# Batch 0 of a fused attention and GEGLU kernel in a new hand-written order, with a longer ring of exponentials and one pair's operands by DMA transposes

## The chip, the core and the metric

The kernel runs on one core of one Trainium2 chip. Its time is the device time in microseconds of one execution, as the median of several runs. The core's engines are TensorE (PE: matrix products and transposes into PSUM; PEld is its loading of stationary operands), VectorE (DVE), ScalarE (ACT), GpSimd (POOL) and SyncE (SP). Each works through its own instructions in their written order, and they wait for each other by semaphores. DMAs that SP issues run in queue q1 of the profile, those that POOL issues in q0.

## The reference

A hash-bucketed attention over 4 batches, 8 heads, 768 positions and a head dimension of 64, followed by a gated feed-forward layer on the 3072 x 512 result:

```python
q_bits = (np.einsum('bhsd,dk->bhsk', q, proj) > 0)      # 6 bits; k_bits alike
mask = q_bucket[:, :, :, None] == k_bucket[:, :, None, :]
scores = np.where(mask, scale * np.matmul(q, k.transpose(0, 1, 3, 2)), -1e9)
attn = softmax(scores)                                  # + 1e-9 in the divisor
x = np.matmul(attn, v)                                  # heads side by side: 3072 x 512
g = x @ w_gate
ffn = (0.5 * g * (1 + erf(g / sqrt(2)))) * (x @ w_val) @ w_out
out = x + ffn / (1 + np.exp(-(x @ w_res)))
```

## The kernel before

The attention is worked in 16 pairs of heads, four to a batch (p = 0 to 15). A pair's q and k are loaded as fp32 (`load`, L75), turned in 32 x 32 blocks by DVE (`tr`, L190), hashed by small fp32 products (`hash_mm`, L197, or `hash_one`, L230, for the first pair), turned back (`hash_tok`, L209) and compared with zero (`bits`, L220). The six bits stand as plus or minus a half beside the 64 columns of a bf16 copy (`cast`, L176) in one of four buffers `nat`; the copy of q is scaled by 1/2048, so that after the product one exponential with a large scale gives both the bucket mask and the score. The operand with its bits is transposed into `aug`: in batch 0 by TensorE (`turn_pe`, L253: six 128 x 128 transposes for one head of one side, into a PSUM bank, and `turned`, L262, copies it out), later by one DMA transpose for both heads (`turn`, L245).

A pair has nine chunks (36 slots to a batch). `scores` (L373) makes a chunk of 128 x 1024 scores in one of two PSUM buffers `sp` and has ACT write its exponential to `e`, a ring of four. `values` (L345) multiplies a chunk's exponentials with v into the PSUM tile `av`; after half of a pair's chunks one head is complete, gets a small uniform term (`preset`, L323, from the sums that `vals_s` makes on POOL) and is divided into `x_tok` (`finish`, L299, on DVE). `finish` also issues a DMA transpose of `x_tok` into `x_sb` for the first two pairs of batch 0; `x_turn` (L335) does the other two on TensorE.

When a batch's attention is done, `gate_val` (L403) makes 12 steps m of gate and value products: both go through the two `sp` buffers, ACT takes the Gelu of the first into `gt`, and DVE multiplies it with the second into `hh` (L419), which frees the second buffer. Work for the next batch's pairs hangs on these steps (`gv_work`). `project` (L425) is spread over the next batch's slots.

The order around all this is written out with slot numbers: `pe(s, ...)` puts a piece behind the scores of slot s, `at(s, ...)` behind the values, `gv(b, m, ...)` behind step m; `loads` and `load_w` (weights, issued by POOL with a cast from fp32, L168) are pieces too. Values follow their scores by two slots (`LAG`). In PSUM, `hash_mm`, q's transposes and the residual products take the bank tagged "r", k's transposes, `htp` and the output products the bank "f".

The lines that set the order of loads, and those in the gate phase of batch 0 for pairs 6 and 7:

```python
loads(s0 + (6 if b == 0 else 2) + 4 * j, (x[0], "qk"[x[1]]))    # x: pairs 4, 5
loads(s0 + (22 if b == 0 else 18) + 3 * j, (y[0], "qk"[y[1]]))  # y: pairs 6, 7
gv(b, 0, lambda p0=p0: tokens((p0, p0 + 1), True))
for m, x in zip((0, 1, 2, 4), xs):
    lay(b, m, x)                                                # bits, then turn
gv(b, 3, lambda y=ys[2]: tr(*y))
gv(b, 5, lambda y=ys[3]: tr(*y))
```

Of the kernel before, what the change touches and what calls it, by code (L numbers as in the profile page):

```python
# [14 lines left out]


@with_exitstack
def kernel(
# [86 lines left out]
    load(1, 0)  # L105
    load_v(0)
    load(1, 1)
    for p in range(2, 4):
        load_v(p - 1)
        load(p, 0)  # L110
        load(p, 1)
# [76 lines left out]
    t32, hsum, htok = {}, {}, {}  # L188

# [7 lines left out]
    def hash_mm(jobs, dhs=(0, 1), hs_=(0, 1)):  # L197
        if jobs[0] not in hsum:
            hsum[jobs[0]] = mm_ps.tile([P, HT, 32], FP32, tag="r", name="hs")
        hs = hsum[jobs[0]]  # L200
        for hh in hs_:
            sl = slice(hh * T, hh * T + T)
            for dh in dhs:
                for j, x in enumerate(jobs):
                    nc.tensor.matmul(hs[32 * j:32 * j + 32, sl], projw[:, dh, :],  # L205
                                     t32[x][:, sl, dh, :], start=(dh == 0), stop=(dh == 1),
                                     tile_position=(0, 32 * j))

    def hash_tok(jobs, psum=False):  # L209
        n = 32 * len(jobs)  # L210
        if psum:
            ht = mm_ps.tile([P, HT, 32], FP32, tag="f", name="htp")
        else:
            ht = sm_pool.tile([P, HT, 32], FP32, tag="ht", name="ht")
        nc.vector.transpose(ht[:n].rearrange("p c n -> p (c n)"),  # L215
                            hsum[jobs[0]][:n].rearrange("p c n -> p (c n)"))
        for j, x in enumerate(jobs):
            htok[x] = (ht, j)

    def bits(p, side, engs=(nc.vector,)):  # L220
        x = (p, side)
        ht, j = htok.pop(x)
        for a in range(4):
            engs[a % len(engs)].tensor_scalar(  # L224
                nat_of(x)[32 * a:32 * a + 32, :, D:D + NBITS],
                ht[32 * j:32 * j + 32, :, NBITS * a:NBITS * (a + 1)], 0.0, 0.5,
                op0=ALU.is_gt, op1=ALU.subtract)


    def hash_one(p, side, hi, pool, tag):  # L230
        hs = pool.tile([P, 2, T, 32], FP32, tag=tag, name="hs1")
        sl = slice(hi * T, hi * T + T)
        for dh in range(2):
            nc.tensor.matmul(hs[:, 0], projs[:, dh, :], t32[p, side][:, sl, dh, :],
                             start=(dh == 0), stop=(dh == 1))
        hsum[p, side, hi] = hs

    def bits_one(p, side, hi):
        hs = hsum.pop((p, side, hi))
        nc.vector.transpose(hs[:, 1].rearrange("p c n -> p (c n)"),  # L240
                            hs[:, 0].rearrange("p c n -> p (c n)"))
        nc.vector.tensor_scalar(nat_of((p, side))[:, hi * T:hi * T + T, D:D + NBITS],
                                hs[:, 1, :, 0:NBITS], 0.0, 0.5, op0=ALU.is_gt, op1=ALU.subtract)

# [7 lines left out]

    def turn_pe(p, side, hi, tag=None, pool=mm_ps):  # L253
        x = (p, side)
        if x not in aug:
            aug[x] = aug_pool.tile([P, HT, P], BF16, tag=f"aug{side}", name=f"aug{side}")
        pt = pool.tile([P, T, P], BF16, tag=tag or "rf"[side], name="pt")
        for t in range(T):
            nc.tensor.transpose(pt[0:KA, t, :], nat_of(x)[:, hi * T + t, 0:KA], ident)  # L259
        pts[p, side, hi] = pt  # L260

    def turned(p, side, hi, eng, t0=0, t1=T):  # L262
# [4 lines left out]
        else:  # L267
            eng.tensor_copy(dst, pt)

# [29 lines left out]
    def finish(p, hi):  # L299
# [4 lines left out]
        o = av.pop((p, hi))  # L304
        rec = sm_pool.tile([P, T], FP32, tag="rec", name="rec")
# [3 lines left out]
        if hi == 1 and (0 < b < B - 1 or hp < HP - (2 if b == 0 else 1)):  # L309
# [6 lines left out]
    def opened(p, hi):  # L316
        if (p, hi) in av:
            return
        av[p, hi] = av_ps.tile([P, T + 1, D + 1], FP32, tag="av", name="av")
# [15 lines left out]
    def x_turn(b, hp):  # L335
        pt = mm_ps.tile([P, T, P], BF16, tag="f" if b == 0 else "r", name="pt")
# [8 lines left out]
    def values(p, c, e):  # L345
        va = vaug[p]
        for i in range(2):
# [12 lines left out]
            if (2 * c + i + 1) % NCH == 0:  # L360
                if p < HP:
                    preset(p, hi)
                if (p, hi) not in late:
                    finish(p, hi)

    pending = []
    late = ((0, 0), (0, 1), (1, 0))
# [5 lines left out]
    def scores(p, c):  # L373
# [10 lines left out]
        e = e_pool.tile([P, 1024], BF16, tag="e", name="e")  # L384
# [5 lines left out]
    hidden = {}  # L390
# [12 lines left out]
    def gate_val(b, begun, beside):  # L403
        for m in range(KF):
            ps = []
            for i, w in enumerate((wg, wv)):
# [5 lines left out]
                if m == 0 and i == 1:  # L412
                    beside()
# [3 lines left out]
            if m == 0:  # L417
# [7 lines left out]
    def project(b):  # L425
        hh = hidden[b]
        for t in range(T):
            last = b == B - 1 and t == T - 1
            rps = mm_ps.tile([P, DMODEL], FP32, tag="r", name="rps")
# [8 lines left out]
            for k0, k1 in ((0, 3), (3, 4)) if last else ((0, KM),):  # L438
                cs = slice(k0 * P, k1 * P)
                if b < B - 1:  # L440
                    fps = mm_ps.tile([P, DMODEL], FP32, tag="f", name="fps")
# [22 lines left out]
    tr(0, 0, 1, 2)  # L464
# [44 lines left out]
    for p in range(HP, NPAIR):  # L509
        for hi, s in enumerate((9 * p - (p % HP == 0), 9 * p + 5)):  # L510
            at(s - 2, lambda p=p, hi=hi: opened(p, hi))
# [23 lines left out]


    at(0, lambda: bits_one(0, 0, 1), lambda: tr(1, 0), lambda: bits_one(0, 1, 1))
    pe(0, lambda: hash_one(0, 1, 1, av_ps, "av"))
    at(1, lambda: tr(1, 1))
    pe(2, lambda: turn_pe(0, 0, 1, "av", av_ps), lambda: turn_pe(0, 1, 1))  # L540
    at(2, lambda: turned(0, 0, 1, nc.vector))
    at(2, lambda: turned(0, 1, 1, nc.vector, 0, 2), lambda: turned(0, 1, 1, nc.vector, 2, T))
    at(2, lambda: tr(2, 0))
    hash_pe((1,), 4, (4,))
    turns_pe(1, (6, 6, 8, 9))
    at(6, lambda: finish(0, 0), lambda: tr(2, 1))
    at(8, lambda: tr(3, 0))
    at(9, lambda: tr(3, 1))
    at(11, lambda: finish(0, 1))
    at(5, lambda: vals_a(1))  # L550
    at(7, lambda: vals_s(1))
    for side in range(2):
        at(4 + side, lambda side=side: cast(2, side, nc.gpsimd))
        at(9 + side, lambda side=side: cast(3, side, nc.gpsimd))
    hash_pe((2, 3), 13, (13, 16))
    turns_pe(2, (15, 15, 17, 18))
    at(15, lambda: finish(1, 0))
    at(13, lambda: vals_a(2))
    at(15, lambda: vals_s(2))
    turns_pe(3, (22, 22, 23, 24))  # L560
    at(18, lambda: vals_a(3))
    at(22, lambda: vals_s(3))
    pe(30, lambda: x_turn(0, HP - 2))
    for i in range(6):
        at(11 + 3 * i, load_w)
    for m in (0, 0, 4, 5, 6, 7):
        gv(0, m, load_w)
    loads(0, (3, "v"))

# [4 lines left out]
    for b in range(B - 1):  # L574
# [3 lines left out]
        for j, (x, y) in enumerate(zip(xs, ys)):  # L578
            at(s0 + 24 + 2 * j, lambda x=x: tr(*x))
            at(s0 + 25 + 2 * j, lambda x=x: cast(*x, nc.gpsimd))  # L580
            if j < 2:
                at(s0 + 32 + 2 * j, lambda y=y: tr(*y))
            loads(s0 + (6 if b == 0 else 2) + 4 * j, (x[0], "qk"[x[1]]))
            loads(s0 + (22 if b == 0 else 18) + 3 * j, (y[0], "qk"[y[1]]))
        gv(b, 0, lambda p0=p0: tokens((p0, p0 + 1), True))
        for m, x in zip((0, 1, 2, 4), xs):
            lay(b, m, x)
        gv(b, 3, lambda y=ys[2]: tr(*y))
        gv(b, 5, lambda y=ys[3]: tr(*y))
        for m, y in zip((5, 5, 6, 6), ys):  # L590
            gv(b, m, lambda y=y: cast(*y, nc.gpsimd))
        gv(b, 6, lambda p0=p0: hashed((p0 + 2, p0 + 3)))
        gv(b, 7, lambda p0=p0: tokens((p0 + 2, p0 + 3), True))
        for m, y in zip((7, 8, 9, 10), ys):
            lay(b, m, y)
    for p in range(HP, NPAIR):
        at(9 * p - 8, lambda p=p: vals_s(p), lambda p=p: vals_a(p))
        loads(9 * p - 20, (p, "v"))
# [13 lines left out]
    for s in range(LAST):  # L612
# [5 lines left out]
        if b >= 1:  # L618
            mlp_mm(AHEAD + (slot + 1) * (NMM - HELD - AHEAD) // NSLOT - done[0])
# [5 lines left out]
        if slot == NSLOT - 1:  # L625
            values(*pending.pop(0))
            ps = (HP * (b + 1), HP * (b + 1) + 1)
            if b == 0:
                nc.scalar.activation(table, warm[:, 0:1], AF.Gelu)
                begun = [gv_mm(0, 0, wg, 0, KM - 1)]  # L630
                values(*pending.pop(0))
                begun.append(gv_mm(0, 0, wv, 0, KM - 1))
                x_turn(b, HP - 1)
                hashed(ps, 0, 3)
                gate_val(b, begun, lambda: hashed(ps, 3, 4))
            else:
                mlp_mm(4)
                flush()
                begun = [gv_mm(b, 0, w, 0, KM - 1) for w in (wg, wv)]
                if b < B - 1:  # L640
                    mlp_mm(NMM)
                    gate_val(b, begun, lambda: hashed(ps))
                else:
                    x_turn(b, HP - 1)
                    mlp_mm(HELD - 7)
                    gv(b, 0, lambda: mlp_mm(NMM))
                    gate_val(b, begun, lambda: mlp_mm(3))
# [35 lines left out]
```

## Time and profile before

| | us |
|---|---|
| time, median of 3 runs (lowest to highest) | 346.99 (346.71 to 347.24) |
| span of the profiled execution, first to last instruction | 344.9 |
| PE busy | 334.2 |
| ACT busy | 206.7 |
| DVE busy | 191.4 |
| POOL busy | 86.3 |
| first exponential of batch 0 starts | 8.49 |
| first Gelu of batch 0 starts | 51.39 |

The profile is one execution. Its page gives the busy time of each engine, and views of the trace give instructions in order of time, groups of equal instructions, what ended each idle time, the chain of waits that ended last, the busy times by stretch and the DMA transfers with the time from issue to landing. A matrix product's end is modelled, so PE's busy share is no measure of how well it is used. Engines that wait for something off the chain cost nothing by it.

### The profile page before, as it was taken

The page shows a single profiled execution, that of the slowest core. Times are in us where ns is not written, and L with a number is a line of the kernel's source. Part 1 is how long each engine was busy: PE and PEld are TensorE (multiplying, and loading weights), DVE is VectorE, ACT ScalarE, POOL GpSimd, SP SyncE. Part 2 cuts the span into 40 slices and gives each one's busy share as a digit, 9 for nine tenths or more (in the row PEclk, how much of TensorE's full clock was granted, in tenths as well). Part 3 has the DMA queues.
Part 4 walks back from the last instruction along what each step waited for, and adds up shares of the span by engine and source line. Part 5 has one row for each costly group of instructions (what it writes and reads, how often), then busy time and mean ns, then how long its engine had stood idle before and what let it go on. Part 6 is the DMA issues. An engine that isn't in the chain of part 4 may idle for free.

```text
span 344.9 us, 7549 instructions
## 1 busy us (share of the span) xinstructions
PE 334.2 (97%) x3064; PEld 204.3 (59%) x3112; DVE 191.4 (56%) x403; ACT 206.7 (60%) x232; POOL 86.3 (25%) x162
## 2 busy tenths in 40 slices
PE   7999999999999999999999999999999999999994
PEld 5667665655666655655666665655566665656442
DVE  7877757755345856757344784747244444333333
ACT  3789973226999962224999982323999984223110
POOL 4779940371055000270044100242030000000000
PEclk9999999999999999999999999999999999999999
DMA  7979999999375833528366642626330220000022
GB/s 224 376 62 219 205 276 217 197 139 193 103 188 172 204 106 78 102 38 149 82 193 188 231 115 65 128 48 113 72 100 32 55 55 30 32 1 0 32 77 76
DMA packets 71171, 42.90 MB, mean 124 GB/s; under 512 B 49504, under 2 KB 68192, under 8 KB 71136
## 3 DMA queue, kind: packets, MB, share of 16 engines
q1 hardware_dynamic: 64720, 37.17, 42.9%
q0 software_dynamic: 6336, 5.24, 10.8%
q8 instruction: 24, 0.39, 0.4%
q14 instruction: 11, 0.09, 0.1%
q10 hardware_dynamic: 80, 0.00, 0.0%
HBM read 29.36 MB, written 6.29 MB: 103 GB/s over the span
## 4 chain that ended last, share of the span: by engine, by line
PE 88%; ACT 4%; DVE 2%; DMA 2%; issue 2%; SPq 1%; POOL 0%; DVEq 0%; ACTq 0%
PE sp L399 36%; PE fps L445 18%; PE sp L380 15%; PE av L354 8%; PE rps L431 6%; ACT e L385 4%; PE hs L205 3%; DMA ld<-in_k_dram 2%; PE pt L259 1%; DVE o L451 1%; DVE nat L224 0%; SPq L96 0%; DVE o L448 0%; DVE ht L215 0%; DVE hh L419 0%
## 5 line engine op out<-in xcount | busy, mean ns | idle before, releaser
L385 ACT ACTIVATE e<-sp 128x1024 bf16<-128x1024 f32 x144 | 143.6, 1027 | 13.5 <-PE sp L380 8.0
L416 ACT ACTIVATE gt<-sp 128x768 bf16<-128x768 f32 x48 | 38.9, 811 | 92.5 <-PE sp L399 92.5
L380 PE MATMUL sp<-aug,aug 71*128 71x256 bf16 (+1 forms) x384 | 86.1, 325 | 1.1 <-ACT e L385 0.6
L445 PE MATMUL fps<-wo,hh 128*128 128x512 bf16 (+2 forms) x274 | 74.7, 369 | 1.6
L419 DVE TENSOR_TENSOR hh<-gt,sp 128x768 bf16<-128x768 bf16 x48 | 45.8, 954 | 50.1 <-PE sp L399 46.1
L399 PE MATMUL sp<-x_sb,wv 128*128 128x512 bf16 (+1 forms) x379 | 70.6, 325 | 0.4 <-DVE hh L419 0.2
L399 PE MATMUL sp<-x_sb,wg 128*128 128x256 bf16 (+1 forms) x373 | 70.4, 324 | 0.7
L354 PEld LDWEIGHTS <-e 128*128 128x128 bf16 x1152 | 53.3, 97 | 28.9 <-issue 1.2
L354 PE MATMUL av<-va,e 128*128 128x65 bf16 x1152 | 58.7, 193 | 0.1
L399 PEld LDWEIGHTS <-wv 128*128 128x128 bf16 x384 | 37.6, 98 | 25.1 <-issue 0.3
L399 PEld LDWEIGHTS <-wg 128*128 128x128 bf16 x384 | 36.8, 98 | 26.2 <-issue 2.3
L445 PEld LDWEIGHTS <-hh 128*128 128x128 bf16 x300 | 27.4, 97 | 22.7 <-issue 0.2
L448 DVE SCALAR_TENSOR_TENSOR o<-th,fps 128x512 f32<-128x512 f32 (+2 forms) x25 | 16.6, 666 | 36.6 <-PE fps L445 31.0
L380 PEld LDWEIGHTS <-aug 71*128 71x128 bf16 x384 | 29.4, 97 | 10.9 <-issue 2.2
L184 POOL TENSOR_SCALAR nat<-ld 128x768 bf16<-128x768 f32 (+1 forms) x16 | 13.8, 861 | 78.0 <-DMA aug<-nat 74.6
L281 POOL TENSOR_TENSOR v<-ldv 128x384 f32<-128x384 f32 x16 | 16.0, 999 | 67.7 <-DMA ldv<-in_v_dram 67.6
L194 DVE STREAM_TRANSPOSE t<-ld 128x768 f32<-128x768 f32 (+1 forms) x34 | 31.0, 916 | 1.4 <-DMA ld<-in_q_dram 0.7
L333 DVE COPY av<-av 128x390 f32<-128x390 f32 x24 | 13.6, 567 | 29.8 <-PE av L329 29.8
L431 PE MATMUL rps<-wr,x_sb 128*128 128x512 bf16 x90 | 25.3, 378 | 0.2
L435 ACT ACTIVATE th<-rps 128x512 f32<-128x512 f32 x24 | 14.2, 594 | 18.4 <-PE rps L431 18.4
L224 DVE TENSOR_SCALAR nat<-htp 32x72 bf16<-32x72 f32 x96 | 21.9, 229 | 1.8
L307 DVE TENSOR_TENSOR x_tok<-av,rec 128x384 bf16<-128x384 f32 x32 | 17.8, 557 | 1.1
(61 smaller groups left out, 190.7 us busy)
## 6 DMA issues: line engine op xcount, KB each, us to landing
ldv<-in_v_dram SPq DMA_DIRECT2D x16, 384.0 KB, 5.4
out_dram<-o SPq DMA_DIRECT2D x23, 256.0 KB, 2.0
ld<-in_q_dram SPq DMA_DIRECT2D x15, 384.0 KB, 5.4
ld<-in_k_dram SPq DMA_DIRECT2D x15, 384.0 KB, 6.2
wg<-in_moe_w_gate_dram POOLq DMA_DIRECT2D x4, 384.0 KB, 10.2
wv<-in_moe_w_val_dram POOLq DMA_DIRECT2D x4, 384.0 KB, 12.2
wo<-in_moe_w_out_dram POOLq DMA_DIRECT2D x3, 512.0 KB, 6.9
wr<-in_moe_w_res_dram POOLq DMA_DIRECT2D x1, 512.0 KB, 14.9
```

The source lines that it names most:

```text
L194: nc.vector.transpose(t32[p, side][:, sl].rearrange("p c h n -> p (c h n)"), raw[p, side][:, sl].rearrange("p c d -> p (c d)"))
L224: engs[a % len(engs)].tensor_scalar(nat_of(x)[32 * a:32 * a + 32, :, D:D + NBITS], ht[32 * j:32 * j + 32, :, NBITS * a:NBITS * (a + 1)], 0 ...
L307: nc.vector.tensor_mul(x_tok[b][:, hp, :, hi * D:(hi + 1) * D], o[:, 0:T, 0:D], rec.unsqueeze(2).to_broadcast([P, T, D]))
L354: nc.tensor.matmul(av[p, hi][:, qt, :], e[:, off:off + P], va[:, hi, jt, 0:D + 1], start=first, stop=(p >= HP and jt == T - 1), skip_group ...
L380: nc.tensor.matmul(sp[:, off:off + nq * P], ks[0:KA, hi * T + jt, :], qs[0:KA, hi * T + qt0:hi * T + qt0 + nq, :], start=True, stop=True)
L385: nc.scalar.activation(e, sp, AF.Exp, scale=float(ALPHA))
L399: nc.tensor.matmul(sp[:, c0:c1], w[:, kk, bass.ts(m, P)], xs[:, kk, c0:c1], start=(kk == 0), stop=(kk == KM - 1))
L416: nc.scalar.activation(gt, sp[:, 0:S], AF.Gelu)
L419: nc.vector.tensor_mul(hidden[b][:, m, :], gt, ps[1][:, 0:S])
L431: nc.tensor.matmul(rps, x_sb[b][:, kk, t, :], wr[:, kk, :], start=(kk == 0), stop=(kk == KM - 1))
L445: nc.tensor.matmul(fps[:, cs], hh[:, m, bass.ts(t, P)], wo[:, m, cs], start=(m == 0), stop=(m == KF - 1))
L448: nc.vector.scalar_tensor_tensor(o[:, cs], th[:, cs], 1.0, fps[:, cs], op0=ALU.add, op1=ALU.mult)
```

## The change

Batch 0's attention leaves the slot loop. Every piece of work gets a name: `s5` and `v5` are the scores and values of chunk 5, `tr41` is `tr` of pair 4, side 1 (k), `h10` to `h13` the four pieces of the second hash, `tk` its turning back, `bt` the comparisons, `tp` and `td` TensorE's transposes and their copies out, `tu` a DMA transpose, `cs` a cast, `ld` and `lv` loads, `va` and `vs` the preparation of v, `w` a weight load, `fin` a finish, `xt` an `x_turn`, `g0` and `g1` the begun first gate and value products. One list gives their order, a second one the pieces beside the 12 steps of batch 0's gate phase. The slot loop starts at batch 1.

```diff
+FIRST_LOADS = [(1, "q"), (0, "v"), (1, "k"), (2, "q"), (2, "k"), (2, "v"), (1, "v"), (3, "k"), (3, "q")]
+HASHES = [(0, (1,)), (1, (2, 3)), (2, (4, 5)), (3, (6, 7))]
+X_PE = 2
+ORDER = """
+trq trk ld41 s0 tdq tdk hoq bo0 ho s1 bo1 tr10 s2 tr11 tp011 cs21 tp001 v0 v1 s3 td011a td011b h00
+h01 td001 s4 s5 h02 h03 ld40 s6 v2 v3 tr20 s7 tr21 v4 tk0 bt10 bt11 tp100 tp110 td100 td110 s8 tr31
+tp111 tr30 lv3 s9 fin00 tp101 td101 ld61 s10 ld50 cs20 v5 v6 v7 v8 fin01 s11 ld51 va2 s12 cs31 h10
+va1 h11 td111 s13 vs1 lv4 h12 h13 s14 v9 v10 cs30 w0 s15 v11 v12 s16 tk1 bt20 bt21 bt31 tp200 tp210
+td200 td210 bt30 tr50 s17 tp201 td201 va4 s18 w1 w2 v13 fin10 vs2 s19 tu31 tp211 td211 cs41 s20 v14
+vs3 s21 v15 tu30 s22 v16 tr40 tr61 v17 s23 tr41 va3 fin11 w3 s24 v18 vs4 s25 v19 v20 v21 s26 cs40
+s27 ld70 v22 v23 fin20 tr51 s28 v24 v25 ld60 s29 v26 fin21 s30 lv5 s31 v27 s32 v28 v29 v30 w4 w5 w6
+cs50 cs51 s33 xt2 s34 v31 fin30 tr60 s35 gelu v32 v33 v34 g0 v35 fin31 g1 xt3 h20 h21 h22 lv6 w7
+op40
+"""
+BESIDE = [
+    "h23 tk2 bt41 tu41 cs61",
+    "bt40 tu40 cs60",
+    "bt50",
+    "bt51 w8 w9 ld71 tr71",
+    "tr70",
+    "tu51 cs71",
+    "h30 h31 h32 h33 tk3 bt61 tu61 tu50",
+    "bt60 w10",
+    "w11",
+    "bt71 tu71",
+    "bt70 cs70 tu70",
+    "pr40 rp40 tu60",
+]
```

The exponentials of batch 0 go to a ring of nine in the tile `hh`, which is free until the gate phase, and TensorE's work takes whichever of the banks "r" and "f" is free:

```diff
+    free_banks, held_banks = ["r", "f"], {}
+    def take(what=None):
+        tag = free_banks.pop(0)
...
+    RING = KF * S // 1024
...
-        e = e_pool.tile([P, 1024], BF16, tag="e", name="e")
+        if p < HP:
+            if 0 not in hidden:
+                hidden[0] = hh_pool.tile([P, KF, S], BF16, tag="hh", name="hh")
+            n = (p * NCH + c) % RING
+            e = hidden[0].rearrange("p m s -> p (m s)")[:, n * 1024:(n + 1) * 1024]
+        else:
+            e = e_pool.tile([P, 1024], BF16, tag="e", name="e")
         nc.scalar.activation(e, sp, AF.Exp, scale=float(ALPHA))
```

At the start, the second head's hash and transposes stand in the list, and ACT copies four of the six blocks of the first operand, DVE the other two. Pair 3 is in the list with `tu30` and `tu31` and without `tp3..`, so its operands come from two DMA transposes:

```diff
-    tr(0, 0, 1, 2)
     cast(0, 0, nc.scalar, 0, 1)
     cast(0, 1, nc.gpsimd, 0, 1)
     bits_one(0, 0, 0)
     turn_pe(0, 0, 0)
     fill(2, 256)
-    turned(0, 0, 0, nc.scalar)
     bits_one(0, 1, 0)
+    turned(0, 0, 0, nc.scalar, 0, 4)
     turn_pe(0, 1, 0)
-    hash_one(0, 0, 1, av_ps, "av")
-    tr(0, 1, 1, 2)
     turned(0, 1, 0, nc.vector, 0, 2)
-    turned(0, 1, 0, nc.vector, 2, T)
...
+    job("gelu", lambda: nc.scalar.activation(table, warm[:, 0:1], AF.Gelu))
+    for i, w in enumerate((wg, wv)):
+        job(f"g{i}", lambda w=w: begun.append(gv_mm(0, 0, w, 0, KM - 1)))
+    for name in ORDER.split():
+        first.pop(name)()
...
+            for m, names in enumerate(BESIDE):
+                for name in names.split():
+                    gv(b, m, first.pop(name))
...
+    gate_val(0, begun)
+    mlp.append(project(0))
+    for s in range(NSLOT, LAST):
```

Batches 1 to 3 keep their order; of pairs 4 to 7 it is the loads, hashes, casts and transposes made during batch 0 that are placed anew.

More of the change, by code (lines that the diff above doesn't have):

```diff
@@ L104 @@
     load_head(0, 1, 1, nc.sync)
[L105 to L111, printed above, removed]
+    for what in FIRST_LOADS:
+        load_v(what[0]) if what[1] == "v" else load(what[0], "qk".index(what[1]))
     warm = const.tile([P, P], BF16, name="warm")
@@ L188, with give, acc, acc_done @@
     t32, hsum, htok = {}, {}, {}
+    free_banks, held_banks = ["r", "f"], {}
+    def take(what=None):
+        tag = free_banks.pop(0)
+        if what is None:
+            free_banks.append(tag)
+        else:
+            held_banks[what] = tag
+        return tag
+    def give(what):
+        if what in held_banks:
+            free_banks.append(held_banks.pop(what))
+    accs = []
+    def acc(what):
+        assert len([x for x in accs if x is not None]) < 2 and (len(accs) < 2 or accs[-2] is None), accs
+        accs.append(what)
+    def acc_done(what):
+        accs[len(accs) - 1 - accs[::-1].index(what)] = None
     def tr(p, side, h0=0, h1=2):
@@ L222, in bits @@
         ht, j = htok.pop(x)
+        n, what = ht_left.pop(id(ht))
+        if n > 1:
+            ht_left[id(ht)] = (n - 1, what)
+        else:
+            give(what)
         for a in range(4):
@@ L411, in gate_val @@
                 ps.append(sp)
-                if m == 0 and i == 1:
+                if m == 0 and i == 1 and beside:
                     beside()
@@ L558, with job @@
[L558 to L568, printed above, removed]
+    first = {}
+    def job(name, fn):
+        first[name] = fn
+    held = []
+    for c in range(HP * NCH):
+        job(f"s{c}", lambda c=c: held.append(scores(*divmod(c, NCH))))
+        job(f"v{c}", lambda: values(*held.pop(0)))
@@ new lines @@
+    for p in range(HP - 1, 2 * HP):
+        job(f"lv{p}", lambda p=p: load_v(p))
+        for side in range(2):
+            job(f"ld{p}{side}", lambda p=p, side=side: load(p, side))
+    for n, ps in HASHES:
+        for i in range(4):
+            job(f"h{n}{i}", lambda i=i, ps=ps: hashed(ps, i, i + 1))
+        job(f"tk{n}", lambda ps=ps: tokens(ps, ps[0] >= HP))
+    for i in range(12):
+        job(f"w{i}", load_w)
+    for hp in range(HP):
+        job(f"xt{hp}", lambda hp=hp: x_turn(0, hp))
@@ L571, in lay @@
+    for what, fn in (("op", opened), ("pr", preset), ("rp", repeat)):
+        job(f"{what}{HP}0", lambda fn=fn: fn(HP, 0))
+    begun = []
+    job("gelu", lambda: nc.scalar.activation(table, warm[:, 0:1], AF.Gelu))
[3 more added lines that the diff above has]
+        first.pop(name)()
     def lay(b, m, x):
```

165 lines of the change are left out of this document (91 added, 74 removed).

## The prediction, made before the changed kernel had run

> **What bounds the kernel now.** I read the page's engine sums first, then the busy times by stage, then ScalarE's timeline through batch 0, because the change touches batch 0 and little else.
>
> ```profile
> PE 334.2 (97%) x3064; PEld 204.3 (59%) x3112; DVE 191.4 (56%) x403; ACT 206.7 (60%) x232; POOL 86.3 (25%) x162
> ```
> ```profile
> 13.39:47.49 34.10, 32.70 (x477) 23.35 (x474) 25.54 (x58) 30.48 (x32) 28.68 (x50) 1.00 1.06 200
> 47.49:51.39 3.90, 3.85 (x51) 2.37 (x51) 1.45 (x4) 1.87 (x3) 0.00 (x0) 1.00 1.18 277
> 51.39:82.56 31.17, 30.85 (x215) 18.41 (x218) 20.60 (x47) 10.17 (x13) 10.32 (x18) 1.00 1.12 189
> ```
>
> The columns after the stretch are its length and the busy time of PE, PE's weight loads, DVE, ACT and POOL, then PE's clock and the share of the DMA engines. PE is at 97% over the span. Batch 0's attention (8.49 to 47.49) is the place where PE is not the plain limit: ACT, PE and, above 1.0, the DMA engines are all close to full. From 51.39 to 82.56 (batch 0's gate and value products) PE sets the time, with the DMA engines still full.
>
> ```profile
> 8.49 4.08 ACT L385 ACTIVATE e<-sp 128x1024 bf16<-128x1024 f32 x4 [0.89 <-PE sp L380]
> 13.39 1.02 ACT L385 ACTIVATE e<-sp 128x1024 bf16<-128x1024 f32 x1 [0.82 <-PE sp L380]
> 14.95 1.94 ACT L385 ACTIVATE e<-sp 128x1024 bf16<-128x1024 f32 x2 [0.54 <-PE sp L380]
> 17.60 5.64 ACT L385 ACTIVATE e<-sp 128x1024 bf16<-128x1024 f32 x6 [0.71 <-PE sp L380]
> 23.72 1.02 ACT L385 ACTIVATE e<-sp 128x1024 bf16<-128x1024 f32 x1 [0.49 <-PE sp L380]
> 25.30 1.94 ACT L385 ACTIVATE e<-sp 128x1024 bf16<-128x1024 f32 x2 [0.55 <-PE sp L380]
> 27.99 6.55 ACT L385 ACTIVATE e<-sp 128x1024 bf16<-128x1024 f32 x7 [0.76 <-PE sp L380]
> 34.80 2.04 ACT L385 ACTIVATE e<-sp 128x1024 bf16<-128x1024 f32 x2 [0.26 <-PE sp L380]
> 37.00 10.47 ACT L385 ACTIVATE e<-sp 128x1024 bf16<-128x1024 f32 x11 [0.16 <-PE sp L380]
> 51.39 0.81 ACT L416 ACTIVATE gt<-sp 128x768 bf16<-128x768 f32 x1 [1.16 <-PE sp L399]
> ```
>
> These 36 exponentials end at 37.00 + 10.47 = 47.47, and the first Gelu comes 3.92 later. Back to back they follow each other by (10.47 - 1.03) / 10 = 0.944 us. The eight gaps in brackets after the first row add up to 4.29 us: that is what a better order can win, plus whatever the first exponential (8.49) can be moved forward. The chain of waits shows what makes a gap.
>
> ```profile
> 14.12 0.59 DVE ht L215
> 15.39 0.20 DVE nat L224
> 15.64 1.01 PE pt L259 x12
> ...
> 16.78 0.17 PE av L326
> ...
> 17.50 0.25 PE av L354 x8
> 17.75 0.44 PE sp L380 x3
> 18.18 0.35 PE pt L259 x6
> ...
> 22.05 0.79 PE hs L205 x16
> ```
>
> A hash goes through DVE (14.12 to 15.59, transpose and six comparisons) while PE holds a 12-fold transpose behind it, in order; the scores stand behind that. The rows also give PE's prices: scores of one chunk 0.44, values 0.25, six transposes 0.35, two hash pieces 0.79, a preset 0.17.
>
> **The change, part by part.** *Removed.* The fourth pair's 24 TensorE transposes (4 x 0.35 = 1.4 us of PE) and four DVE copies:
>
> ```profile
> L268 DVE COPY aug<-pt 71x768 bf16<-71x768 bf16 x13 | 6.7, 542 | 2.2 <-PE pt L259 2.2
> ```
>
> 4 x 0.54 = 2.2 us of DVE. With them gone PE's work from piece s4 to s35 is 32 x 0.44 + 30 x 0.25 + 8 x 0.35 + 6 x 0.40 (hash pieces) + 7 x 0.17 + 0.35 (xt2) = 28.3 us, against 32 x 0.944 = 30.2 us of ACT. So ACT sets the pace there and I book the 1.4 us at nothing by itself: it is cover for the lumps. The ring of nine lets values lag by up to six chunks (s26 is issued when v21 is done); the old ring of four with two in hand could not.
>
> *Start.*
>
> ```profile
> 6.57 0.57 DVE L194 STREAM_TRANSPOSE t<-ld 128x384 f32<-128x384 f32 x1
> 7.15 0.87 PE L234 MATMUL hs<-t,projs 128*128 128x192 f32 x4
> 7.35 0.62 DVE L268 COPY aug<-pt 71x256 bf16<-71x256 bf16 x2 [0.22 <-PE pt L259]
> 7.86 0.60 PE L380 MATMUL sp<-aug,aug 71*128 71x512 bf16 x2
> 11.42 0.20 POOL projw L144
> ```
>
> The first scores (7.86) stood behind a hash of the second head on PE (7.15), and the first comparisons behind a 0.57 transpose on DVE. Both now come after. DVE's first copy moves from 7.35 to about 6.8, s0 to 7.05, the first exponential to 7.05 + (8.49 - 7.86) = 7.7: 0.8 earlier. But s1 now waits for two transposes and two copies on DVE (2 x 0.5 + 0.2 + 0.4 after 6.9, so 8.5), which puts the second exponential at 9.55, a gap of 0.9. The first pair's hash still waits for projw (11.62), two pieces (0.79) and s4 follow it, so the fifth exponential starts at 13.2 against 13.39: a gap of 0.6 and another of 0.15 before it.
>
> *Middle.* Counting PE and DVE forward by the order with the prices above, I find three more gaps that the order leaves: 0.5 at s8 (tk0 and its six comparisons end at 16.15, then 2 x 0.35 and the scores), 0.5 at s11 (v5 to v8 and a preset are 1.17, more than 0.944 - 0.44), and 0.25 in small ones up to s17. Sum of gaps 2.9 in place of 4.29. The last exponential ends at 7.7 + 35 x 0.944 + 1.03 + 2.9 = 44.7 (2.7 earlier). Bounds: with the start's gaps alone (1.65) it is 43.4; with as much as now (4.29) it is 46.1.
>
> *The fourth pair's DMA transposes.* tu31 is ready when its comparisons end, about 26.0, tu30 about 27.8; s27 wants both by 7.7 + 27 x 0.944 + 2.9, less the 0.7 by which scores lead their exponential, that is 35.4. Ahead of them on SP's queue stand x_sb's first transpose, ld51 and lv4; behind them x_sb's second, ld70, ld60, lv5, lv6.
>
> ```profile
> L248 SPq DMA_TRANSPOSE aug<-nat x8: 1433/1682/5029, 54.8 to 82.1; - x8
> ...
> DMA to landing us min/median/max: 3.7/4.1/9.7
> ```
> ```profile
> ldv<-in_v_dram SPq DMA_DIRECT2D x1, 384.0 KB, 7.7
> ```
> ```profile
> q0 software_dynamic: 378, 0.28, 93.7%
> q1 hardware_dynamic: 422, 0.11, 41.1%
> ```
> ```profile
> q1 hardware_dynamic: 1971, 0.50, 123.2%
> ```
>
> The 7.7 is v4's load issued at 25.22 today; its twin lv4 is issued near 24.5, so it lands at 30 to 32. The q rows are 36 to 38 us (weights in q0 against a transpose in q1) and 64 to 66 (transposes alone). An operand is 128 x 12 x 128 x 2 bytes in packets of 256, so 1536 packets: 1.6 us alone (985 per us), 7.3 us beside weights (211 per us). Both transposes alone need 3.1 us after lv4, so 33 to 35, in time; POOL's va4 also waits for lv4 and holds w1 and w2 back, which gives them that window. Bounds: no wait, or 3.5 us (the second rival). I take 0.3, near the lower end, because of that window.
>
> *Tail.* v35, preset, g1, xt3 and three hash pieces follow the last exponential much as now; 3.84 in place of 3.92. First Gelu: 44.7 + 0.3 + 3.84 = 48.9, that is 2.5 earlier.
>
> *Gate phase.* k7's load (ld71) moves from slot 31 to the fourth step of the gate, on SP behind tu41 and tu40, and tr71 needs it at once; behind tr71 on DVE stands the hh product of step 4, which frees PSUM for the next value product, so PE stops about 0.3 us after DVE is late.
>
> ```profile
> 54.82 28.71 SPq L248 DMA_TRANSPOSE aug<-nat  x8
> ```
> ```profile
> 56.10 0.95 DVE L224 TENSOR_SCALAR nat<-htp 32x72 bf16<-32x72 f32 x4
> ...
> 60.32 0.95 DVE L419 TENSOR_TENSOR hh<-gt,sp 128x768 bf16<-128x768 bf16 x1 [0.66 <-PE sp L399]
> 61.19 0.97 DVE L194 STREAM_TRANSPOSE t<-ld 128x768 f32<-128x768 f32 x1
> 62.92 0.95 DVE L419 TENSOR_TENSOR hh<-gt,sp 128x768 bf16<-128x768 bf16 x1 [0.76 <-PE sp L399]
> ```
> ```profile
> ld<-in_q_dram SPq DMA_DIRECT2D x1, 384.0 KB, 3.4
> ```
>
> Relative to the first Gelu (51.39): first transpose issued +3.4, second ready +5.7, step 4's product +11.5. So in the new kernel tu41 is issued at 52.3, tu40 is ready at 54.6, tr71 wants its data at 59.8 (after step 3's product and four comparisons) and step 4 is due at 60.4. The load can be issued once tu40 is off SP: 54.6 + 1.43 at the earliest, 3.77 + 5.03 after 52.3 (the first two issues today) at the latest, and then takes 3.4 alone: 59.5 to 64.5. Weights w4 to w7, issued some 45 to 47, keep q0 full to about 56 and slow tu41, so that tu40's packets end near 59.5 and the load lands about 61.3. Then step 4 starts at 62.4: 2.0 late, 1.6 of it paid by PE (0.3 is slack, 0.1 the late comparisons). Bounds 0 and 4.9.
>
> The remaining pieces (w8 to w11, tu61 to tu60, the opening of pair 4) have 10 us or more before their use: nothing.
>
> **Sum** against the profiled execution (span 344.9, 2.1 less than the median of the runs): -2.7 + 0.3 - 0.1 + 1.6 = -0.9, span 344.0, time 346.1.
>
> **Rivals.**
> (a) The load lands before 59.8, so only the first part counts: -2.5, **344.5**. For it: a lone load took 3.4 and 1.43 is the shortest issue. Against: it needs both transposes through in 5 us while q0 is full. Chance 0.22.
> (b) The fourth pair's transposes are late at s27. w1 and w2 are 512 packets each; sharing turn by turn, 1024 transpose packets go at 211 per us (4.9 us), the other 2048 at 985 (2.1 us): 31 + 7 + 0.9 = 38.9, 3.5 after 35.4. The gate then starts 0.7 later than now and its load is less late (0.5): **348.2**. It decides as soon as w1's packets start before tu31's end. The Trainium skill ("DMA: Bandwidth & Descriptors", section "Queues, rings and completion order") says that a DMA engine takes packets in turn from the queues that have work; the 378 beside 422 above agree. By that rule alone the sum is this rival's wherever the weights overlap the transposes. Chance 0.14.
> (c) Slower: tu41 and tu40 hold SP for 3.77 and 5.03 as today, the load is issued at 61.1 and lands at 64.5, step 4 starts at 65.5 against 62.92 now: +2.3, **349.3**, and more where the load queues longer. From a landing after 62 on it eats the whole gain. For it: the first two issues today were under the same weights. Against: fewer weights are left at that time. Chance 0.22.
> (d) The order only moves the gaps (4.29 remain): the attention ends 1.3 earlier, the load is then 0.8 late for PE, and -1.3 + 0.3 - 0.1 + 0.8 = -0.3: **346.7**, no change. Chance 0.08.
>
> **Numbers.** Forecast 346.1, chance 0.34, its own range 345 to 347.2. What a measurement can tell from no change is 0.2%, 0.7 us. Faster: all of (a), two thirds of the forecast: 0.44. Within: a quarter of the forecast and (d): 0.17. Slower: (b), (c) and the rest: 0.39. The range 343.8 to 350 leaves out a better (a) with fewer gaps, and (c) with a long queue.
>
> **What would show it.** Right: first exponential near 7.7, gaps of the exponentials near 2.9 in sum, the last ending near 45, no PE wait for a DMA at s27, first Gelu near 49, and one DVE wait for ld<-in_k_dram in the gate of 1 to 2 us with PE idle behind it. Wrong: a PE wait on aug at the fourth pair's first scores (b), a wait of 4 us or more in the gate (c), none (a), or exponentials with gaps as now (d). A late ld60 ahead of the attention's last product, which I book at nothing since it should land near 42 and is wanted near 44, would also break it.

## The result and the profile after

| | median us | lowest to highest | executions | ratio to before (95% interval) |
|---|---|---|---|---|
| before | 346.84 | 346.36 to 347.46 | 20 | |
| changed | 348.92 | 345.31 to 350.63 | 20 | 1.0049 (1.0031 to 1.0067) |

The changed kernel is 0.5% slower where the forecast was 346.1, slightly faster. Its spread is five times that of before, and its profiled execution is the shortest of the twenty (345.31, span 343.6): this profile shows what the change can do and hides most of what costs it the time. So I read it first against the steps of the prediction, and then the profile of a longer execution of the same kernel (348.48, span 346.8, the run e_look1 below).

The windows of the changed kernel, with the columns explained in the prediction: attention, its tail, and the gate phase from the first Gelu to the twelfth; the last row is the gate phase of the kernel before.

```profile
8.03:45.08 37.05, 36.09 (x507) 25.40 (x508) 27.61 (x65) 34.26 (x36) 28.51 (x55) 1.00 1.04 248
45.08:48.99 3.91, 3.86 (x51) 2.38 (x51) 1.29 (x4) 1.87 (x4) 2.39 (x4) 1.00 1.26 223
48.99:80.51 31.52, 29.75 (x207) 17.64 (x210) 19.68 (x43) 8.91 (x12) 5.41 (x7) 1.00 1.15 182
```
```profile
51.39:81.29 29.90, 29.58 (x207) 17.62 (x210) 19.89 (x44) 8.92 (x11) 10.32 (x18) 1.00 1.12 188
```

From the first exponential to the end of the last are 37.05 us; before it was 47.47 - 8.49 = 38.98. The tail is as long as it was. The gate phase took 29.90 before and takes 31.52 now, so 1.6 of the gain went there. ScalarE's timeline through batch 0's attention shows the gaps, in brackets:

```profile
8.03 1.02 ACT L459 ACTIVATE hh<-sp 128x1024 bf16<-128x1024 f32 x1 [1.05 <-PE sp L448]
9.98 1.94 ACT L459 ACTIVATE hh<-sp 128x1024 bf16<-128x1024 f32 x2 [0.92 <-PE sp L448]
12.11 1.02 ACT L459 ACTIVATE hh<-sp 128x1024 bf16<-128x1024 f32 x1 [0.19 <-PE sp L448]
13.42 3.77 ACT L459 ACTIVATE hh<-sp 128x1024 bf16<-128x1024 f32 x4 [0.29 <-PE sp L448]
17.66 2.91 ACT L459 ACTIVATE hh<-sp 128x1024 bf16<-128x1024 f32 x3 [0.46 <-PE sp L448]
21.00 2.85 ACT L459 ACTIVATE hh<-sp 128x1024 bf16<-128x1024 f32 x3 [0.44 <-PE sp L448]
24.10 20.98 ACT L459 ACTIVATE hh<-sp 128x1024 bf16<-128x1024 f32 x22 [0.24 <-PE sp L448]
```

Six gaps of 2.54 in sum in place of eight of 4.29; from 24.10 on, 22 exponentials follow each other without one, chunk 27 with pair 3's DMA transposes among them. VectorE's timeline and PE's waits in the gate phase show the late load that was foreseen:

```profile
58.91 0.98 DVE L282 TENSOR_SCALAR nat<-htp 32x72 bf16<-32x72 f32 x4
61.15 0.98 DVE L240 STREAM_TRANSPOSE t<-ld 128x768 f32<-128x768 f32 x1 [1.26 <-DMA ld<-in_k_dram]
62.16 0.95 DVE L492 TENSOR_TENSOR hh<-gt,sp 128x768 bf16<-128x768 bf16 x1
```
```profile
PE sp L472 <- DVE hh L492: 1.5, 1, 1.5
```

k7's load lands at 61.15, DVE waits 1.26 for it, and PE 1.5 behind DVE. SP's timeline has tu41 and tu40, and the load behind them, which landed 3.6 later:

```profile
52.41 5.11 SPq L308 DMA_TRANSPOSE aug<-nat  x2
57.57 0.57 SPq L107 DMA_DIRECT2D ld<-in_k_dram  x1
```

Now the longer execution of the same kernel: the waits of DVE and PE (us in total, times, longest) in its gate phase and the turn to batch 1.

```profile
DVE nat L282 <- DMA aug<-nat: 3.4, 1, 3.4
...
PE fps L518 <- DVE nat L282: 1.5, 1, 1.5
...
PE sp L472 <- DVE hh L492: 0.8, 1, 0.8
...
PE sp L448 <- DVE hh L492: 0.6, 1, 0.6
DVE t L240 <- DMA ld<-in_k_dram: 0.6, 1, 0.6
```

The load costs less here (0.6, and 0.8 of PE). The long wait is another one: DVE's comparisons `bt70` (line 282 writes `nat`) wait 3.4 us for a DMA transpose, and with them the last product of the gate, on which the first output product (line 518) and the scores (line 448) hang. In the short execution this wait was 0.83; the kernel before has none. VectorE's timeline of the long execution, and ScalarE's at the turn to batch 1 in the short execution, in the long one and in the kernel before:

```profile
84.29 0.96 DVE L282 TENSOR_SCALAR nat<-htp 32x72 bf16<-32x72 f32 x4 [3.36 <-DMA aug<-nat]
85.28 0.95 DVE L492 TENSOR_TENSOR hh<-gt,sp 128x768 bf16<-128x768 bf16 x1
```
```profile
82.63 1.02 ACT L459 ACTIVATE e<-sp 128x1024 bf16<-128x1024 f32 x1
83.55 0.59 ACT L508 ACTIVATE th<-rps 128x512 f32<-128x512 f32 x1
84.03 2.87 ACT L459 ACTIVATE e<-sp 128x1024 bf16<-128x1024 f32 x3
```
```profile
83.33 1.02 ACT L459 ACTIVATE e<-sp 128x1024 bf16<-128x1024 f32 x1
84.25 0.59 ACT L508 ACTIVATE th<-rps 128x512 f32<-128x512 f32 x1
86.92 3.00 ACT L459 ACTIVATE e<-sp 128x1024 bf16<-128x1024 f32 x3 [2.08 <-PE sp L448]
```
```profile
83.42 1.02 ACT L385 ACTIVATE e<-sp 128x1024 bf16<-128x1024 f32 x1
```

The second exponential follows the first by 1.40 in the short one and by 3.59 in the long one. Against before (span 344.9) the long span is made up so: first exponential 0.84 later, attention 1.85 shorter, gate phase 0.93 longer (30.83), and 1.99 more from batch 1's first exponential to the end (263.47 against 261.48): +1.9. The short execution needs 260.97 for that last part. The wait for one transpose thus costs 2.5 us in this execution. The other profiles of the changed order agree, the variants below among them: the last part is 260.7 to 261.1 in the eight where DVE waits 0.83 or less for tu50, and 262.3 to 263.5 in the five where it waits 2.5 to 3.4.

The timelines of GpSimd and SP, and the landing of SP's two transposes issued between 72 and 74 (the first is tu61, the second tu50), show where it comes from in the long execution:

```profile
60.74 0.80 POOL L193 DMA_DIRECT2D wr<-in_moe_w_res_dram  x1
61.55 0.75 POOL L193 DMA_DIRECT2D wo<-in_moe_w_out_dram  x1
71.75 0.82 POOL L210 CAST nat<-ld 128x768 bf16<-128x768 f32 x1 [9.46 <-DMA aug<-nat]
72.53 1.49 POOL L193 DMA_DIRECT2D wo<-in_moe_w_out_dram  x2
```
```profile
61.42 27.18 SPq L308 DMA_TRANSPOSE aug<-nat  x6
```
```profile
L308 SPq DMA_TRANSPOSE aug<-nat x2: 1414/3068/4721, 71.1 to 72.6; - x2
...
  DVE nat L282: 3.4, 1
...
DMA to landing us min/median/max: 3.7/7.7/11.7
```

tu51 goes out at 61.42, between w8 and w9 (60.74, 61.55), shares the engines with their packets and lands after 10.2. GpSimd's cast cs71 waits 9.46 for it, and w10 and w11, which stand behind cs71 on GpSimd, go out from 72.53 on, at the same moment as tu50 (72.6). So tu50 meets 1 MB of weights and lands after 11.7 us, at 84.3. The DMA queues from 77 to 82:

```profile
q0 software_dynamic: 771, 0.77, 91.6%
q1 hardware_dynamic: 768, 0.20, 30.4%
```

771 packets of weights and 768 of transposes, one for one: at that rate an operand of 1536 packets takes 10 us. The Trainium skill ("DMA: Bandwidth & Descriptors", section "Queues, rings and completion order") says that a DMA engine takes packets in turn from the queues that have work; these rows agree.

Which course an execution takes goes with a race between tu51 and w8. In the five profiles where tu51 went out first (by 0.1 to 1.3 us; 60.03 against 60.55 in the short execution) it landed in 3.7 to 7.5, and w10 and w11, where they were not moved, went out by 69.0 and met tu61. In the eight where w8 was first, tu51 took 10.1 to 13.3, and they went out at 71.5 or later. No run changed this order alone.

### The profile page after: what moved, and what is told of

Read it like the earlier page. It is cut to its first block, busy times and chain, and to the rows that moved or that the text cites. A ratio compares the mean times of both kernels' runs of the same rounds, so it can differ in the third digit from the quotient of the medians.

```text
span 343.6 us, 7501 instructions
## 1 busy us (share of the span) xinstructions
PE 332.7 (97%) x3040; PEld 202.5 (59%) x3088; DVE 188.5 (55%) x400; ACT 206.2 (60%) x232; POOL 85.5 (25%) x162
## 4 chain that ended last, share of the span: by engine, by line
PE 90%; ACT 4%; DVE 2%; issue 2%; DMA 1%; SPq 1%; POOL 0%; DVEq 0%; ACTq 0%; POOLq 0%
PE sp L472 33%; PE fps L518 18%; PE sp L448 17%; PE av L421 9%; PE rps L504 6%; PE hs L251 3%; ACT hh L459 3%; PE pt L320 1%; DMA ld<-in_k_dram 1%; PE wps L174 1%; DVE hh L492 1%; SPq L308 1%; PE hs L293 1%; PE pt L405 0%; PE av L396 0%
## 5 line engine op out<-in xcount | busy, mean ns | idle before, releaser
L459 ACT ACTIVATE e<-sp 128x1024 bf16<-128x1024 f32 x108 | 109.1, 1027 | 8.2 <-PE sp L448 2.8
L472 PE MATMUL sp<-x_sb,wv 128*128 128x256 bf16 (+1 forms) x378 | 70.6, 325 | 1.9 <-DVE hh L492 1.6
L472 PE MATMUL sp<-x_sb,wg 128*128 128x512 bf16 (+1 forms) x374 | 70.4, 324 | 0.6
L421 PEld LDWEIGHTS <-e 128*128 128x128 bf16 x864 | 40.2, 97 | 25.1
L421 PE MATMUL av<-va,e 128*128 128x65 bf16 x864 | 43.4, 193 | 0.0
L459 ACT ACTIVATE hh<-sp 128x1024 bf16<-128x1024 f32 x36 | 34.3, 1030 | 3.8 <-PE sp L448 3.6
```

What stands on the lines that cost most here:

```text
L421: nc.tensor.matmul(av[p, hi][:, qt, :], e[:, off:off + P], va[:, hi, jt, 0:D + 1], start=first, stop=(p >= HP and jt == T - 1), skip_group ...
L459: nc.scalar.activation(e, sp, AF.Exp, scale=float(ALPHA))
L472: nc.tensor.matmul(sp[:, c0:c1], w[:, kk, bass.ts(m, P)], xs[:, kk, c0:c1], start=(kk == 0), stop=(kk == KM - 1))
```

## The experiments

Theories named in the expectations: **late load** (k7's load, as forecast), **late operands** (DMA transposes that land late: pair 3's at chunk 27, or tu50 at the end of the gate phase), **clock** (a lower granted clock). Later, A is DVE's wait for tu50, B the late load, C the contention of w10 and w11 with tu50. The ratio is to executions of the kernel before on the same chip; e_same, e_ld71, e_pe3 and e_both ran on one chip (346.70 before), the others on a second (346.79, and 347.02 from e_nat5 on).

**e_same: the changed kernel again, for its spread.**

> The changed kernel once more, for a second profiled execution and more times. The profiled one (345.3) is the fastest of 20 that reach to 350.6, so its reading (one stall of 1.5 us of PE in the gate phase) can't be that of the median. Late load (ld71 behind two DMA transposes): a slower execution shows DVE waiting 3 to 6 us for ld<-in_k_dram at step 4 of the gate, attention ending near 45 as before. Late operands (the fourth pair's two DMA transposes): the attention itself ends 2 to 5 us later, with PE waiting for DMA aug<-nat at chunk 27. Clock: neither wait is longer, and the granted clock is lower in some stretch. Median 347 to 350.

347.87 (345.64 to 349.02), ratio 1.0027 (1.0009 to 1.0045): still slower. In its profile (346.8) the load's wait is 0.7, and DVE's for DMA aug<-nat has grown from 0.83 to 2.9. That was the first sign of tu50.

**e_ld71: k7's load early.**

```diff
-... h20 h21 h22 lv6 w7
+... h20 h21 h22 lv6 ld71 w7
-    "bt51 w8 w9 ld71 tr71",
+    "bt51 w8 w9 tr71",
```

> The changed kernel with k7's load issued ahead of tu41 and tu40, at the end of the attention, in place of behind them. Late load: DVE's wait at step 4 is gone, the median falls to 344 to 345 and the spread to about 1 us. Late operands or clock: the median stays above 346.5 and the spread at 3 us or more, though the profiled execution is 1.5 us shorter than the first one in the gate phase.

345.24 (344.47 to 348.25), ratio 0.9963 (0.9943 to 0.9982). The wait for the load is gone, but two of twelve executions are still over 347, and in the profile DVE's wait for tu50 is 0.7. Taken alone this would have "shown" the late load. But the edit also moved w10 and w11: they went out at 65.55 and met tu61 in place of tu50, which landed at 80.6 (issued 74.4, 6.2 later), early enough for most of the wait to go.

**e_pe3: pair 3's transposes back on TensorE.**

```diff
-... s19 tu31 tp211 ... v15 tu30 s22 ... s23 tr41 va3 ... s25 v19 v20 v21
+... s19 tp211 ... v15 s22 ... s23 tp300 tp310 td300 td310 tr41 va3 ... s25 tp301 td301 v19 tp311 td311 v20 v21
```

> The changed kernel with the fourth pair's operands by TensorE transposes and DVE copies again (24 transposes, 1.4 us of PE), the two DMA transposes left out. Late operands: the spread narrows to about 1 us and the median comes to 345 to 346.5 (the load's 1.5 us stays, the gaps of ACT may grow by up to 1 us). Late load: spread and median stay (347 to 350), or the median falls a little since the DMA engines have 800 KB less to move. Clock: no change.

345.71 (345.08 to 346.37), ratio 0.9967 (0.9955 to 0.998). Chunk 27 waited in no profile of the changed kernel, though, and here, too, it is the gate phase that changed. w10 and w11 went out at 74.29, after tu50 (72.8), which landed in 4.1, and DVE has no wait for a DMA left in the gate phase. (TensorE's transposes bring a gap of 0.59 before chunk 26's exponential.)

**e_both: both edits.**

> Both: k7's load early and the fourth pair by TensorE. Late load: as with the load alone, 344 to 345.5. Late operands: as with TensorE's transposes, less 1.5 us, 344 to 345. Clock: still above 346.5 with a wide spread.

345.21 (344.77 to 345.92), ratio 0.9954 (0.994 to 0.9968): no better than the load alone, by the median; the executions over 347 are gone.

Two unlike edits each remove the whole loss. That fits neither theory as it was put, and asks for something that both disturb.

**e_look1, e_look2: the changed kernel again, for profiles.**

> The changed kernel unaltered, once more, for a profile of an execution of ordinary length (its times so far: 345.3 to 350.6). The two profiles so far were of executions of 345.3 and 346.8. Late load: in an execution over 347.5, DVE's wait for k7's load (ld<-in_k_dram) is 3 us or more (1.26 and 0.7 in the two shorter ones), and the first Gelu is near 49 still. Late operands at the scores of chunk 27: PE waits 2 us or more for a DMA aug<-nat and the first Gelu comes after 51. Late operands at the end of the gate phase: DVE's wait for DMA aug<-nat before pair 7's comparisons is 4 us or more (0.83 and 2.9 in the shorter ones). Clock: none of the waits differs and only the clock at the end of the span does.

> As the look before it, a second execution. If it is short (under 347), all three waits are as in the two profiles known: load 0.7 to 1.3, chunk 27 nothing, pair 7's comparisons 0.8 to 2.9. If it is long, the same of the three waits is long as in the first look.

348.48 and 347.21. The first is the long execution shown above. In the second the load's wait is 0.4, chunk 27's nothing, tu50's 3.0; tu50 landed after 11.3. The load's wait is not longer in the longer executions (1.26, 0.7, 0.6 and 0.4 at 345.3, 346.8, 348.5 and 347.2), tu50's is (0.83, 2.9, 3.4, 3.0). The granted clock was 1.00 in both.

**e_tu50: tu50 earlier on SP's queue.**

```diff
-    "tr70",
+    "tr70 tu50",
...
-    "h30 h31 h32 h33 tk3 bt61 tu61 tu50",
+    "h30 h31 h32 h33 tk3 bt61 tu61",
```

> The changed kernel with one piece moved: tu50, the DMA transpose that reads the tile into which pair 7's comparisons bt70 are written four steps later, goes from step 6 of the gate phase to step 4, so that it is issued ahead of tu51 and tu61. The load of k7 and pair 3's DMA transposes stay. Late operands at the end of the gate phase: if that wait is what makes executions of 347.5 and more, the median falls from 347.9 to 346.5 or below. Late load, or late operands at chunk 27: the median stays at 347.5 to 349, since both come before step 4.

345.68 (344.27 to 346.22), ratio 0.9965 (0.9952 to 0.9978). One piece moved gives 2.2 us less than e_same (2.3 when each is taken against its own kernel before), with the late load and pair 3's transposes left in. SP's timeline has tu50 as the first of this row:

```profile
58.95 6.42 SPq L308 DMA_TRANSPOSE aug<-nat  x2
```

It could go out at 58.95, and landed 4.7 later. In the changed kernel's four profiles it went out at 71.6 to 75.3 only because tu61 stands ahead of it, which needs the hash of pairs 6 and 7.

**e_w12: w1 and w2 behind va3.**

```diff
-... va4 s18 w1 w2 v13 fin10 ... tr41 va3 fin11 w3 s24
+... va4 s18 v13 fin10 ... tr41 va3 fin11 w1 w2 w3 s24
```

> The changed kernel with the weight loads w1 and w2 moved from behind s18 to behind va3 (ahead of w3), so that nothing on the weights' queue can lie beside pair 3's two DMA transposes; the same bytes come some 4 us later. Late operands at chunk 27: the median falls to 346 or below and no PE wait for aug is left at chunk 27. Late load: the weights are pressed closer to the gate phase, so tu41, tu40 and the load of k7 land later, and the median stays at 348 or rises to 350.

346.9 (345.7 to 348.65), ratio 1.0004 (0.9986 to 1.0021): neither theory's number. The wait for tu50 is 2.5, that for the load 1.2; PE does not wait at chunk 27, but did not in the changed kernel's profiles either. It says nothing against chunk 27 that these profiles don't.

**e_nat5: a fifth `nat` tile for pair 7's q.**

```diff
-        return nat[(2 * x[0] + x[1]) % NN]
+        return nat[NN] if x == (HP + 3, 0) else nat[(2 * x[0] + x[1]) % NN]
...
+    job("bl", lambda: blank(NN, nc.gpsimd))
...
-    "tr70",
+    "tr70 bl",
```

> The changed kernel with a fifth tile for the natural layout, used by q of pair 7 alone, so that bt70 no longer waits until tu50 has read the tile of pair 5. Nothing else moves (GpSimd fills the tile's constant columns at step 4 of the gate phase). Theory A, DVE's wait for tu50 is the loss: DVE's wait for DMA aug<-nat goes to 0, the second exponential of batch 1 follows the first by 1.4 us again (3.1 to 3.6 in the changed kernel's executions over 346), and the median falls from 347.9 to 345.5 to 346. Theory B, the late load of k7 is the loss: DVE's wait for ld<-in_k_dram stays at 0.4 to 1.3 and the median at 347.5 or above.

345.15 (344.71 to 345.2), ratio 0.9946 (0.9927 to 0.9964). SP's transposes between 71.7 and 74, and VectorE's timeline where it used to wait:

```profile
L308 SPq DMA_TRANSPOSE aug<-nat x2: 1414/3506/5598, 70.5 to 72.0; - x2
...
DMA to landing us min/median/max: 3.7/8.0/12.3
```
```profile
79.34 0.95 DVE L492 TENSOR_TENSOR hh<-gt,sp 128x768 bf16<-128x768 bf16 x1 [0.63 <-PE sp L472]
80.32 0.96 DVE L282 TENSOR_SCALAR nat<-htp 32x72 bf16<-32x72 f32 x4
81.94 0.95 DVE L492 TENSOR_TENSOR hh<-gt,sp 128x768 bf16<-128x768 bf16 x1 [0.66 <-PE av L396]
```

tu50 is as late as ever (72.0 + 12.3 = 84.3, the same instant as in the long execution), but bt70 starts at 80.32 without waiting. It is the reuse of the tile that costs the time, not the operand's lateness: the operand itself is wanted much later (PE waits for no DMA up to 130). The load's wait (0.9, 1.1 of PE) is still there.

**e_w1011: w10 and w11 behind tu50.**

```diff
-    "bt60 w10",
-    "w11",
+    "bt60",
+    "",
     "bt71 tu71",
-    "bt70 cs70 tu70",
+    "bt70 cs70 w10 w11 tu70",
```

> The changed kernel with the last two weight loads, w10 and w11, taken from steps 7 and 8 of the gate phase to step 10, behind cs70, which waits for tu50: their bytes can no longer lie beside tu50's. In the executions with a long wait GpSimd issued both at 71.5 to 72.5, beside tu50 (issued 71.6 to 72.6), which then took 11.2 to 11.7 us to land; in the short one both went out at 67.5 and tu50 took 9.1; where they went out after it (74.3, with pair 3's transposes on TensorE) it took 4.1. Theory C, the contention of w10 and w11 with tu50 is what makes it late: tu50 lands in 3.7 to 5 us, DVE's wait for aug<-nat goes to 0, median 345.5 to 346.5 (up to 0.5 more if the last third of wo comes late to the output products). Theory A alone without C (four steps are too few whatever else is on the queues): the wait stays at 2 to 3 us and the median at 347.5 or above.

345.78 (345.27 to 345.99), ratio 0.9963 (0.995 to 0.9976). The same two transposes, and GpSimd's timeline:

```profile
L308 SPq DMA_TRANSPOSE aug<-nat x2: 1519/1611/1703, 71.0 to 72.5; - x2
...
DMA to landing us min/median/max: 3.7/3.9/4.0
```
```profile
76.71 0.82 POOL L208 TENSOR_SCALAR nat<-ld 128x768 bf16<-128x768 f32 x1 [7.53 <-DMA aug<-nat]
77.50 1.56 POOL L193 DMA_DIRECT2D wo<-in_moe_w_out_dram  x2
```

Issued as late as in the long execution, tu50 lands in 4.0 in place of 11.7 once the weights are out of its way: theory C. (The 9.1 that the expectation gives for the short execution is tu61's. There the weights met tu61, which held SP for 4.81; tu50 went out behind it at 75.3 and landed at 81.0. In both the weights make it late, in one beside it and in the other through the transpose ahead of it.)

**e_tu50late: tu50 one step later.**

```diff
-    "h30 h31 h32 h33 tk3 bt61 tu61 tu50",
-    "bt60 w10",
+    "h30 h31 h32 h33 tk3 bt61 tu61",
+    "bt60 tu50 w10",
```

> The changed kernel with tu50 one step later (step 7 in place of 6), three steps ahead of bt70 in place of four; a step takes 2.6 us. Theory A: DVE's wait grows by up to 2.6 us to 4 to 6, PE's idle time behind it with it, and the median rises to 349.5 to 351. Theory B: 347.5 to 348.5 as the changed kernel. If by the shift w10 and w11 go out ahead of tu50 and are done with when it starts, the wait grows by less than 1 and the median by less than 0.5.

347.17 (346.38 to 351.72), ratio 1.0019 (0.9995 to 1.0043): no longer than e_same's 1.0027. In its profile tu50 went out at 71.9 (71.7 in e_same) and the wait is 3.1. The step under which a DMA is written down is not its time of issue: it stands directly behind tu61 on SP in both lists. That is why A's number (349.5 to 351) did not come.

**e_ld_tu: k7's load early and tu50 early, pair 3 by DMA as in the change.** The edits are those of e_ld71 and e_tu50 together.

> The changed kernel with both repairs that keep its DMA transposes of pair 3: k7's load directly behind lv6 as in the first experiment, and tu50 at step 4 of the gate phase. Theory A: no wait of DVE for a DMA in the gate phase, no execution over 346.5 (two of twelve were with the load alone moved), median 344.5 to 345.3. If the executions over 347 of the moved load come from chunk 27, one or two such executions stay.

344.63 (344.13 to 344.66), ratio 0.9934 (0.9913 to 0.9954): the version that beats both kernels. In its profile DVE waits for no DMA in the gate phase. Two of PE's waits are these, the first at chunk 27 of the attention, the second in the gate phase:

```profile
PE sp L448 <- DMA aug<-nat: 0.3, 1, 0.3
PE sp L472 <- DVE hh L492: 0.2, 1, 0.2
```

## Why the prediction was wrong, point by point

- **Start**, first exponential at 7.7: it came at 8.03, and at 7.95 to 9.49 in the other twelve profiles of the changed order. The copies and scores follow as forecast; what varies is PE's first hash (last section). The kernel before has only one profile, so how its start varies is not shown.
- **Middle**, 2.9 of gaps and 44.7 - 7.7 = 37.0 from the first exponential to the end of the last: 2.54 and 37.05. The gaps at s1, s8 and s11 are there (0.92, 0.46, 0.44); that at s4 is 0.29 in place of 0.6. The mechanism is right; that the length fits so well is in part luck. The sum takes each exponential at 0.944, but one with a gap behind it takes 1.03, 0.08 more: for the kernel before the same sum gives 8.49 + 35 x 0.944 + 1.03 + 4.29 = 46.85 in place of 47.47. Six such breaks make 0.5 here, and the gaps came out 0.4 below the 2.9.
- **Pair 3's DMA transposes at chunk 27**, 0.3: nothing in the changed kernel's profiles, 0.3 in e_ld_tu. Rival (b) falls: w1 and w2 went out at 31.80 and 32.64, but from 32 to 34 q0 moved 10 packets beside 1104 of q1, and tu30 landed at 35.1.
- **Tail**, 3.84: 3.91.
- **k7's load**, landing 61.3 and 1.6 of PE: 61.15 and 1.5 in the short execution, 0.6 to 0.9 of PE in the changed kernel's other three. By the medians it is worth 0.5 (e_nat5 345.15 against e_ld_tu 344.63, which differ otherwise only in how the wait for tu50 is removed) to 1.05 (e_tu50 against e_ld_tu). Rival (c), 64.5, falls: the row of tu41 and tu40 on SP is 5.11 long, not 8.8. Rival (a), a landing before 59.8, falls with the 61.15, and (d), gaps as before, with the 2.54.
- **The step that failed** is the one in which "the remaining pieces (w8 to w11, tu61 to tu60, the opening of pair 4)" were given 10 us or more before their use and booked at nothing. I looked for the use of what a transpose writes. Its other end is the tile that it reads: pair 5's and pair 7's q share one `nat` tile, and bt70 must wait until tu50 has read it. In the long execution bt70 was due at 84.29 - 3.36 = 80.9, only 8.3 after tu50 went out, and tu50 took 11.7. Before, they lay at steps 2 and 9, and pair 5's q was turned ahead of its k and of everything of pair 6; the change put tu50 behind tu51 and tu61 on SP, where w10 and w11 came to lie beside it or beside tu61. I did count SP's queue for the load that moved, and not for the transpose that moved past two others. Term: 0 booked; 2.1 to 2.7 by the medians (e_same 347.87 against 345.78, 345.68 and 345.15 in the three variants that remove it in three ways), or 2.3 to 3.0 with each against its own kernel before; 2.5 in the trace.

With 2.5 for it and 1.0 in place of 1.6 for the load, the sum of the prediction becomes -2.7 + 0.0 - 0.0 + 1.0 + 2.5 = +0.8, and the start, 0.3 to 1.8 later than forecast, makes it +1.1 to +2.6: the medians are +1.2 (e_same against 346.7) and +2.1 (348.92 against 346.84), the second with more of the long executions of the next paragraph. Without both waits it is -2.4 to -0.9; e_ld_tu has -2.4 (344.63 against 347.02), e_both -1.5.

Not settled: the executions over 348.8, eleven of the first twenty, two of e_same's twelve and three of e_tu50late's ten, of which none was profiled. They show a granted clock of 0.988 to 0.995; all shorter ones have 0.997 or more, but for one of e_w12 (348.65 at 0.992). In the short execution's profile the clock falls to 0.5 only from 341.67 on, behind PE's last product, and in the long one's (span 346.8) it does not fall at all. Whether a lower clock costs time in them was not tried, so the 1.05 by which the first median (348.92) lies above e_same's (347.87) is not explained. They came only where the wait was left in. In the 23 executions of the four variants in which bt70 does not wait for tu50 and pair 3 stays with its DMA transposes, the longest is 346.22.

## What to carry to other kernels

A transfer has two ends: when it is moved, look not only at who reads what it writes but at who overwrites what it reads, above all where few tiles go round. Its time of issue is set by what stands ahead on its queue and not by the step it is listed under, and its duration by what shares the DMA engines then. And when two unlike repairs each remove a whole loss, look for a third thing that both shift; a repair by moving a piece is proof only with a second one that leaves the timing alone, as the fifth tile did.

## What the runs showed of the hardware that was not expected

A DMA transpose of 1536 small packets lands in 3.7 to 4.1 us alone and in 9.0 to 13.3 where it lies beside weight loads all the way: the two queues share by packets (771 and 768), so the small ones of the transpose get a fifth of the bytes (0.20 of 0.97 MB).

PE's first hash has no fixed duration. The two rows are PE's timeline of the short and of the long execution:

```profile
4.16 1.54 PE L293 MATMUL hs<-t,projs 128*128 128x192 f32 x8
```
```profile
4.24 2.75 PE L293 MATMUL hs<-t,projs 128*128 128x192 f32 x8
```

The same eight matmuls took 1.54 in four profiles (before, the short execution, e_w12, e_ld_tu) and up to 2.90 (e_tu50), and the first exponential follows: 7.95, 8.03 and 8.06 with 1.54 in the changed order, 9.33 with 2.75, 9.49 with 2.90. That is up to 1.5 us of spread between executions that start alike (1.3 among the changed kernel's own four), as large as most effects here. The Trainium skill ("TensorE: Matmul & The Clock Gate", the section on the HAM clock gate) says that PE starts at half its clock and that the number of slow matmuls differs from run to run; the durations would fit that, but the granted clock of the profile reads 1.00 in this stretch in both executions, so no run here shows the cause.
